# Column halves of the output summed in two TensorE column groups of one bank, two output stores, and w4 in five pieces

## The chip, the cores and the metric

One core of a Trainium2 chip runs the kernel. The metric is device time in microseconds (us) of one execution. Ratios are the mean time of one kernel's fast runs over the mean of the other's fast runs of the same rounds, so they are not quite the ratio of the medians quoted beside them. A profiled execution has a span (first to last instruction) about 1.8 us shorter than the time of the run.

## The reference

One decode step of a block: attention over the last 2,048 positions of a cache (4 batches, 32 query heads, 16 KV heads of 128), plus an MLP, both on the same normalised input, and a residual. What matters here is the last sum:

```python
def reference(...):
    xn = _layernorm(A_x)
    return A_x + attention(xn, K, V, wq) @ wo + mlp(xn, w1, w2, w3, w4)   # shortened
# mlp: x1 + gelu(layernorm(x1) @ w3) @ w4     w4: 4608 x 576, wo: 4096 x 576, output: 4 x 576
```

The weights and the cache window are 87 MB, read once, for 4 rows of output. (The sequence has one position, so the shifted part of the MLP is zero and the kernel leaves w1 and w2 out.)

## The kernel before

K, V, wo, w3 and w4 stream in on SyncE's DMA queue, and w4 comes last. The output is 4 x 576. TensorE's sums stand in PSUM, in banks; the widest matmul in this kernel's trace writes 512 columns, and the 576 columns here are summed as two halves of 288. A chunk is 128 rows of a weight (w4 has 36, wo 32). All wo terms (3 x 8 chunks during the loop and 8 at its end) and all 36 w4 chunks go into `acc`. The halves lie in different rows of the same 32-column group of TensorE: row `2 b + i` is half `i` of batch `b`, and the shifted view of a zero-padded `lhsT` with 8 columns puts half `i` into its rows.

```python
W4_PIECES = [0, NFH, NF - 12, NF - 6, NF - 2, NF - 1, NF]     # 0 18 24 30 34 35 36: six DMAs
...
second = []
def acc_matmuls(terms):
    for i in range(NI):                                       # NI = 2 halves
        for n, (lhsT, rhs) in enumerate(terms):
            to, q, start = (second[0], QD, second[1]) if second and n % 2 else (acc, 0, False)
            nc.tensor.matmul(out=to[q:q + OR, :], lhsT=lhsT[:, NI - 1 - i:NI - 1 - i + OR],
                             rhs=rhs[:, i * CW:(i + 1) * CW], start=start, stop=False, skip_group_check=True)
            ...
# the end of the kernel
acc_odd = ps_acc.tile([P, CW], F32, tag="g", name="acc_odd")  # a second bank, used by column group 1
second += [acc_odd, True]
...                                                            # last attention head
o_proj(hl)
mlp_out(*pieces[0]); ...; mlp_out(*pieces[3])                  # chunks 0 to 33: even -> acc, odd -> acc_odd
second.clear()
odd = const.tile([OR, CW], F32)
nc.scalar.activation(out=odd[:], in_=acc_odd[QD:QD + OR, :], func=ACT.Copy)
seen = const.tile([1, 1], F32)
nc.vector.tensor_copy(out=seen[:], in_=odd[0:1, 0:1])
for lo, hi in pieces[4:]:                                      # chunks 34 and 35, into acc alone
    mlp_out(lo, hi)
fin = const.tile([OR, CW], out.dtype)
nc.vector.tensor_tensor(out=fin[:], in0=acc[0:OR, :], in1=odd[:], op=ALU.add)
nc.sync.dma_start(out=o2.rearrange("b (i n) -> (b i) n", i=NI), in_=fin[:])
```

So in the closing stretch even and odd chunks already run side by side, in column groups 0 and 1, in two banks. Only the last two chunks run in one group, so that the odd sum can be copied out meanwhile.

## Time and profile before

| | before |
|---|---|
| time | 211.74 us (211.57 to 211.84, 3 runs) |
| span, mean granted clock | 209.9 us, 0.89 |
| DMA | 87.31 MB, mean 416 GB/s |
| last landing of w4 | 206.81 us |

From the page of the kernel before, the rows by 40 equal slices of the span. A digit is tenths of a slice; PEclk is the granted TensorE clock, DMA the mean busy share of the core's 16 DMA engines.

```profile
PE   0378198699670039649998999659995976898684
PEclk9999769999996557976999999999997968899969
DMA  8999999999999999999999999999999999999991
```

DMA is at 9 tenths or more from the second slice to the last but one; nothing else is. A change made under that stream cannot show unless it holds the stream up. What can show is the stream itself, and the stretch after its last byte.

The end of the chain of waits of the kernel before (start, length, what), with lines left out:

```profile
168.46 32.19 DMA w_sb<-in_B_w_dram
200.65 0.04 issue
200.70 0.40 PE acc L183
...
206.13 0.27 PE acc L183
...
206.81 0.41 ACT odd L612
207.22 0.02 issue
207.25 0.14 DVE seen L614
```

One w4 transfer, then TensorE to 206.8, then the odd sum. Taken alone it says that TensorE ended the stream. The landings say more. The trace records 16 increments of a semaphore for each of the six transfers; the last of the 16 is called its landing here. The six pieces landed at 200.65, 202.57, 204.69, 206.07, 206.43 and 206.81 us. The timeline of the kernel before (start, length, engine, line, operation, output, inputs, shape, count), in its last stretch:

```profile
206.12 0.29 PE L183 MATMUL acc_odd<-w_sb,gT 128*8 128x288 bf16 x1
206.24 0.28 PE L183 MATMUL acc<-w_sb,gT 128*8 128x288 bf16 x1
206.24 0.29 PE L183 MATMUL acc_odd<-w_sb,gT 128*8 128x288 bf16 x1
...
206.60 0.65 PE L183 MATMUL acc<-w_sb,gT 128*8 128x288 bf16 x4
206.81 0.40 ACT L612 ACTIVATE odd<-acc_odd 8x288 f32<-8x288 f32 x1 [10.46 <-PE acc_odd L183]
207.25 0.14 DVE L614 COPY seen<-odd 1x1 f32<-1x1 f32 x1 [8.54 <-ACT odd L612]
207.32 0.43 DVE L619 TENSOR_TENSOR fin<-acc,odd 8x288 bf16<-8x288 f32 x1
207.78 0.37 SPq L620 DMA_DIRECT2D out_dram<-fin  x1
```

Matmuls start at 200.70, 206.12 and (the third of the four in the line at 206.60) 206.85, each 0.04 us after a landing. So it is the landings that TensorE follows at the end. `acc` and `acc_odd` matmuls start together, 0.12 us from pair to pair (a "slot"). The windows of the kernel before (stretch, length, busy us of PE, PEld, DVE, ACT and POOL, then granted clock, DMA share, GB/s) show that half of this stretch ran at half clock:

```profile
197.00:200.50 3.50, 1.56 (x25) 0.97 (x24) 1.14 (x3) 0.00 (x0) 0.00 (x0) 1.00 0.93 388
200.50:204.00 3.50, 3.30 (x28) 1.90 (x29) 0.00 (x0) 0.00 (x0) 0.00 (x0) 0.51 1.01 422
204.00:206.00 2.00, 2.00 (x34) 1.47 (x31) 0.00 (x0) 0.00 (x0) 0.00 (x0) 1.00 0.71 272
206.00:207.50 1.50, 1.25 (x16) 0.63 (x11) 0.26 (x2) 0.40 (x1) 0.00 (x0) 1.00 0.11 39
```

The clock came back just in time for TensorE to catch up with the stream.

### The profile page before, as it was taken

To read this page: it belongs to the slowest core of one execution; us is meant where nothing else is said; L and a number is where in the kernel's file an instruction comes from. 1 tells how busy PE (TensorE), PEld (TensorE's weight loads), DVE (VectorE), ACT (ScalarE), POOL (GpSimd) and SP (SyncE) were. 2 spreads that over 40 slices of the span, in tenths; PEclk is the share of its full clock that TensorE was granted. 3 is DMA by queue.
4 is the path that set the end of the run, shared out by engine and by line. 5 is a ranking of instruction groups with operands and counts; after the bars stand their busy time and mean duration, and the time that the engine had idled before them with its cause. 6 is when DMAs were issued, how large, how long until landed. Compare 5 with 4: busy or idle time off the path is not lost.

```text
span 209.9 us, 2326 instructions
## 1 busy us (share of the span) xinstructions
PE 149.1 (71%) x941; PEld 60.2 (29%) x955; DVE 113.7 (54%) x165; ACT 34.4 (16%) x66; POOL 8.9 (4%) x33
## 2 busy tenths in 40 slices
PE   0378198699670039649998999659995976898684
PEld 0123032233220013223454333224331312343353
DVE  3611877985910084917507898465949391755200
ACT  7612201021120001111120312110111111113100
POOL 4620000000000000000000300000000000000000
PEclk9999769999996557976999999999997968899969
DMA  8999999999999999999999999999999999999991
GB/s 294 406 403 440 422 428 431 437 425 432 448 429 419 421 437 421 447 418 437 434 425 437 418 426 439 434 423 440 418 431 437 422 433 431 434 428 446 417 399 71
DMA packets 6658, 87.31 MB, mean 416 GB/s; under 512 B 748, under 2 KB 1016, under 8 KB 1656
## 3 DMA queue, kind: packets, MB, share of 16 engines
q1 hardware_dynamic: 6640, 87.17, 97.5%
q8 instruction: 7, 0.11, 0.2%
q10 hardware_dynamic: 8, 0.00, 0.0%
q14 instruction: 3, 0.02, 0.0%
HBM read 87.17 MB, written 0.00 MB: 415 GB/s over the span
## 4 chain that ended last, share of the span: by engine, by line
DMA 52%; PE 24%; DVE 19%; issue 2%; ACT 1%; SPq 0%; DVEq 0%; ACTq 0%
DMA vn<-in_A_v_cache_dram 19%; DMA w_sb<-in_B_w_dram 15%; DVE kt L226 14%; DMA kn<-in_A_k_cache_dram 12%; PE S L342 9%; DMA wq_sb<-in_A_wq_dram 6%; PE acc L183 4%; PE O L394 2%; PE g_ps L460 2%; PE q_ps L286 2%; DVE mx L348 2%; PE S L364 1%; PE oT L407 1%; DVE PT L376 1%; DVE dm L350 1%
## 5 line engine op out<-in xcount | busy, mean ns | idle before, releaser
L342 PE MATMUL S<-kt,qz 128*128 128x512 bf16 x242 | 74.0, 429 | 34.5 <-DVE kt L226 31.3
L226 DVE STREAM_TRANSPOSE kt<-kn 128x2048 int32<-128x2048 int32 x32 | 73.4, 2295 | 26.5 <-DMA kn<-in_A_k_cache_dram 25.0
L342 PEld LDWEIGHTS <-qz 128*128 128x128 bf16 x256 | 24.0, 108 | 63.5 <-issue 46.6
L394 PE MATMUL O<-vn,PT 128*32 128x512 bf16 x256 | 22.9, 400 | 8.4 <-DMA vn<-in_A_v_cache_dram 8.4
L370 ACT ACTIVATE E<-S 128x512 bf16<-128x512 f32 x16 | 9.5, 597 | 97.7 <-PE S L364 97.7
L376 DVE STREAM_TRANSPOSE PT<-E 128x512 bf16<-128x512 bf16 x16 | 11.4, 710 | 15.5 <-ACT E L370 15.5
L401 ACT ACTIVATE O_sb<-O,rd 128x512 f32<-128x512 f32 x16 | 11.0, 686 | 37.1 <-PE O L394 37.1
L394 PEld LDWEIGHTS <-PT 128*32 128x32 bf16 x256 | 5.9, 94 | 29.6 <-issue 28.6
L417 DVE TENSOR_REDUCE on<-oT 128x8 bf16<-128x128 f32 x16 | 4.6, 287 | 16.7 <-PE oT L407 16.6
L348 DVE TENSOR_REDUCE mx<-S 128x1 f32<-128x512 f32 x16 | 10.5, 658 | 1.2 <-PE S L342 1.1
L407 PE MATMUL oT<-ident_w,O_sb 128*128 128x128 f32 x64 | 11.0, 296 | 0.3 <-ACT O_sb L401 0.3
L407 PEld LDWEIGHTS oT<-ident_w,O_sb 128*128 128x128 f32 x64 | 7.0, 146 | 4.6 <-issue 3.9
L183 PE MATMUL acc<-wo_sb,op 128*8 128x288 bf16 x56 | 7.5, 286 | 1.0 <-DVE op L439 1.0
L364 PE MATMUL S<-nm,j_row 8*128 8x512 bf16 x16 | 6.3, 393 | 1.9 <-DVE nm L360 1.7
L183 PE MATMUL acc<-w_sb,gT 128*8 128x288 bf16 x38 | 6.6, 342 | 0.8 <-DMA w_sb<-in_B_w_dram 0.8
L380 PE MATMUL dn<-rs,same_j 128*128 128x1 f32 x32 | 6.4, 268 | 0.0
L380 PEld LDWEIGHTS dn<-rs,same_j 128*128 128x128 f32 x32 | 5.2, 204 | 4.1 <-issue 3.4
L330 PE MATMUL S<-negbig,ohT 4*128 4x512 bf16 x16 | 6.1, 384 | 0.0
L183 PE MATMUL acc_odd<-w_sb,gT 128*8 128x288 bf16 x34 | 6.1, 350 | 0.0
L183 PEld LDWEIGHTS <-op 128*8 128x8 bf16 x64 | 4.6, 87 | 3.2 <-DVE op L439 1.1
L286 PE MATMUL q_ps<-wq_sb,xnT 128*32 128x512 bf16 x40 | 4.5, 630 | 1.3 <-DMA wq_sb<-in_A_wq_dram 1.3
L478 DVE COPY g_x<-gT_ps 128x64 f32<-128x64 f32 (+1 forms) x3 | 0.6, 194 | 8.5 <-PE gT_ps L472 8.5
(93 smaller groups left out, 80.7 us busy)
## 6 DMA issues: line engine op xcount, KB each, us to landing
kn<-in_A_k_cache_dram SPq DMA_DIRECT2D x16, 2048.0 KB, 23.8
vn<-in_A_v_cache_dram SPq DMA_DIRECT2D x16, 2048.0 KB, 25.6
wo_sb<-in_A_wo_dram SPq DMA_DIRECT2D x4, 1152.0 KB, 26.4
w_sb<-in_B_w_dram SPq DMA_DIRECT2D x1, 4608.0 KB, 33.2
wq_sb<-in_A_wq_dram SPq DMA_DIRECT2D x1, 4096.0 KB, 12.8
w_sb<-in_B_w_dram SPq DMA_DIRECT2D x1, 2592.0 KB, 32.2
w_sb<-in_B_w_dram SPq DMA_DIRECT2D x2, 864.0 KB, 34.0
w_sb<-in_B_w_dram SPq DMA_DIRECT2D x2, 576.0 KB, 32.5
```

The costliest lines, as they stand in the source:

```text
L183: nc.tensor.matmul(out=to[q:q + OR, :], lhsT=lhsT[:, NI - 1 - i:NI - 1 - i + OR], rhs=rhs[:, i * CW:(i + 1) * CW], start=start, stop=False ...
L226: nc.vector.transpose(out=kt[:], in_=src)
L286: nc.tensor.matmul(out=q_ps[r][g * QD:(g + 1) * QD, :], lhsT=xnT[:, k, :], rhs=wq_sb[:, col:col + NW], start=(j == 0), stop=False, skip_gr ...
L342: nc.tensor.matmul(out=S_ps[h][:], lhsT=qz[:, z0:z0 + P], rhs=kt[:, ib, c0:c0 + SC, e:2 * QD:2].rearrange("p c k -> p (c k)"), start=False ...
L348: nc.vector.reduce_max(out=mx[:], in_=S_ps[h][:], axis=AX.X)
L364: nc.tensor.matmul(out=S_ps[h][:], lhsT=j_row[:], rhs=st.pop(("nm", h))[:, 0:1].to_broadcast([NJ, NW]), start=False, stop=False, skip_grou ...
L370: nc.scalar.activation(out=E[h][:].rearrange("p c k -> p (c k)"), in_=S_ps.pop(h)[:], func=ACT.Exp, scale=scale, accum_out=rs[:])
L376: nc.vector.transpose(out=PT[h][:], in_=E.pop(h)[:])
L380: nc.tensor.matmul(out=dn[:], lhsT=same_j[:], rhs=st.pop(("rs", h))[:], start=True, stop=True)
L394: nc.tensor.matmul(out=O_ps[h][g * QD:(g + 1) * QD], lhsT=PT[h][:, c, :], rhs=vn[:, :, c, :], start=(s == 0), stop=False, skip_group_check ...
L401: nc.scalar.activation(out=O_sb[h][:], in_=O_ps.pop(h)[:], func=ACT.Copy, scale=st.pop(("rd", h))[:, 0:1])
L407: nc.tensor.transpose(out=oT[:, s, :], in_=o[:, s, :], identity=ident_w[:, s * NJ:s * NJ + P])
```

## The change

The two halves of each chunk go to two column groups, at partitions 0 and 32 of the same bank. No zero-padded operands are needed, no odd sum, no second bank. The copy `fin` then has its rows in partitions 0 to 3 and 32 to 35. The check before the chip refuses one DMA for both (its access pattern may select partitions only in the first dimension), so there are two stores, on SyncE's and ScalarE's queues. With the odd sum gone, w4's second and third pieces are joined.

```diff
-    W4_PIECES = [0, NFH, NF - 12, NF - 6, NF - 2, NF - 1, NF]
+    W4_PIECES = [0, NFH, NF - 6, NF - 2, NF - 1, NF]
...
-    gT = cleared([P, NF, OW], "gT")
-    op = cleared([P, WOR, OW], "op")
+    gT = const.tile([P, NF, B], BF16, name="gT")
+    op = const.tile([P, WOR, B], BF16, name="op")
...
     def acc_matmuls(terms):
-        for i in range(NI):
-            for n, (lhsT, rhs) in enumerate(terms):
-                to, q, start = (second[0], QD, second[1]) if second and n % 2 else (acc, 0, False)
-                nc.tensor.matmul(out=to[q:q + OR, :], lhsT=lhsT[:, NI - 1 - i:NI - 1 - i + OR],
-                                 rhs=rhs[:, i * CW:(i + 1) * CW], start=start, stop=False, skip_group_check=True)
-                if start:
-                    second[1] = False
+        for lhsT, rhs in terms:
+            for i in range(NI):
+                nc.tensor.matmul(out=acc[i * QD:i * QD + B, :], lhsT=lhsT, rhs=rhs[:, i * CW:(i + 1) * CW],
+                                 start=False, stop=False, skip_group_check=True)
...
-    odd = const.tile([OR, CW], F32)
-    nc.scalar.activation(out=odd[:], in_=acc_odd[QD:QD + OR, :], func=ACT.Copy)
-    seen = const.tile([1, 1], F32)
-    nc.vector.tensor_copy(out=seen[:], in_=odd[0:1, 0:1])
-    for lo, hi in pieces[4:]:
+    for lo, hi in pieces:
         mlp_out(lo, hi)
 
-    fin = const.tile([OR, CW], out.dtype)
-    nc.vector.tensor_tensor(out=fin[:], in0=acc[0:OR, :], in1=odd[:], op=ALU.add)
-    nc.sync.dma_start(out=o2.rearrange("b (i n) -> (b i) n", i=NI), in_=fin[:])
+    fin = const.tile([P, CW], out.dtype)
+    nc.vector.tensor_copy(out=fin[:], in_=acc[:])
+    for i, eng in enumerate((nc.sync, nc.scalar)):
+        eng.dma_start(out=o2[:, i * CW:(i + 1) * CW], in_=fin[i * QD:i * QD + B, :])
```

Cut: the padded identity of the first term, and the same edits where `op`, `gT` and their callers use the padded rows.

More of the change, by code (lines that the diff above doesn't have):

```diff
@@ L166 @@
     qz = cleared([P, ZP + Hkv * 4 * P], "qz")
-    OR = NI * B
-    OW = OR + NI
-    ROWS = slice(NI - 1, NI - 1 + OR, NI)
-    gT = cleared([P, NF, OW], "gT")
-    op = cleared([P, WOR, OW], "op")
+    gT = const.tile([P, NF, B], BF16, name="gT")
+    op = const.tile([P, WOR, B], BF16, name="op")
     acc = ps_acc.tile([P, CW], F32)
     nc.vector.memset(acc[:], 0.0)
-    second = []
     def acc_matmuls(terms):
-        for i in range(NI):
-            for n, (lhsT, rhs) in enumerate(terms):
-                to, q, start = (second[0], QD, second[1]) if second and n % 2 else (acc, 0, False)
-                nc.tensor.matmul(out=to[q:q + OR, :], lhsT=lhsT[:, NI - 1 - i:NI - 1 - i + OR],
-                                 rhs=rhs[:, i * CW:(i + 1) * CW], start=start, stop=False, skip_group_check=True)
-                if start:
-                    second[1] = False
+        for lhsT, rhs in terms:
+            for i in range(NI):
+                nc.tensor.matmul(out=acc[i * QD:i * QD + B, :], lhsT=lhsT, rhs=rhs[:, i * CW:(i + 1) * CW],
+                                 start=False, stop=False, skip_group_check=True)
     def layernorm(dst_f, dst_bf, src):
@@ L268 @@
     nc.vector.reduce_sum(out=own[:], in_=ident_f[:].rearrange("p (h d) -> p h d", h=WOH), axis=AX.X)
-    idz = const.tile([B, OW], F32)
-    nc.gpsimd.memset(idz[:], 0.0)
-    nc.gpsimd.tensor_copy(out=idz[:, ROWS], in_=ident_f[0:B, 0:B])
     xsum = xn_f
     nc.gpsimd.tensor_tensor(out=xsum[:], in0=xn_f[:], in1=x_bf[:], op=ALU.add)
-    acc_matmuls([(idz[:], xsum)])
+    acc_matmuls([(ident_f[0:B, 0:B], xsum)])
     ln2_bf = part(D, B)
@@ L438, in o_pick @@
         with nc.allow_low_precision("one term is not zero"):
-            nc.vector.reduce_sum(out=op[:, :, ROWS], in_=mk[:].rearrange("p i h b -> p i b h"), axis=AX.X)
+            nc.vector.reduce_sum(out=op[:], in_=mk[:].rearrange("p i h b -> p i b h"), axis=AX.X)
     def o_proj(h):
@@ L443, in o_proj @@
             return
-        for i in range(0, WOR, 2):
-            acc_matmuls([(op[:, i + u, :], wo_tiles[h // WOQ][:, i + u, :]) for u in range(2)])
+        acc_matmuls([(op[:, i, :], wo_tiles[h // WOQ][:, i, :]) for i in range(WOR)])
     G_CHUNKS = [(e, 4 * g, 4) for e in range(2) for g in range(NQD)] + [(e, 16, 2) for e in range(2)]
@@ L486, in mlp_act @@
         nc.gpsimd.tensor_scalar(out=u[:], in0=u[:], scalar1=0.5, scalar2=0.5, op0=ALU.mult, op1=ALU.add)
-        nc.gpsimd.tensor_tensor(out=gT[:, :, ROWS], in0=u[:], in1=xs[:], op=ALU.mult)
+        nc.gpsimd.tensor_tensor(out=gT[:], in0=u[:], in1=xs[:], op=ALU.mult)
     def mlp_out(lo, hi):
         w4 = w_tiles["w4"]
-        for i in range(lo, hi, 2):
-            acc_matmuls([(gT[:, u, :], w4[:, u, :]) for u in range(i, min(i + 2, hi))])
+        acc_matmuls([(gT[:, u, :], w4[:, u, :]) for u in range(lo, hi)])
     order = [("K", 0), ("K", 1), ("K", 2)]
@@ L598 @@
     pieces = list(zip(W4_PIECES, W4_PIECES[1:]))
-    acc_odd = ps_acc.tile([P, CW], F32, tag="g", name="acc_odd")
-    second += [acc_odd, True]
     o_turn(hl)
@@ L605 @@
     o_proj(hl)
-    mlp_out(*pieces[0])
-    mlp_out(*pieces[1])
-    mlp_out(*pieces[2])
-    mlp_out(*pieces[3])
-    second.clear()
-    odd = const.tile([OR, CW], F32)
-    nc.scalar.activation(out=odd[:], in_=acc_odd[QD:QD + OR, :], func=ACT.Copy)
-    seen = const.tile([1, 1], F32)
-    nc.vector.tensor_copy(out=seen[:], in_=odd[0:1, 0:1])
-    for lo, hi in pieces[4:]:
+    for lo, hi in pieces:
         mlp_out(lo, hi)
-    fin = const.tile([OR, CW], out.dtype)
-    nc.vector.tensor_tensor(out=fin[:], in0=acc[0:OR, :], in1=odd[:], op=ALU.add)
-    nc.sync.dma_start(out=o2.rearrange("b (i n) -> (b i) n", i=NI), in_=fin[:])
+    fin = const.tile([P, CW], out.dtype)
+    nc.vector.tensor_copy(out=fin[:], in_=acc[:])
+    for i, eng in enumerate((nc.sync, nc.scalar)):
+        eng.dma_start(out=o2[:, i * CW:(i + 1) * CW], in_=fin[i * QD:i * QD + B, :])
 _INS = ['A_x', 'A_k_cache', 'A_v_cache', 'A_wq', 'A_wo', 'B_x', 'B_w1', 'B_w2', 'B_w3', 'B_w4']
```

## The prediction

> **What bounds the kernel now.** The page's slices show DMA at 9 tenths nearly everywhere, mean 416 GB/s; the chain of waits is 52% DMA, from 168.5 us one w4 transfer, then tail. The trace's semaphore landings put the six w4 pieces at 200.65, 202.57, 204.69, 206.07, 206.43 and 206.81 us, and the timeline shows matmuls starting 0.04 us after three of them (200.70, 206.12, 206.85). TensorE ran at half clock from 200.6 to 204.0 (windows view: 0.50), but had caught up: the last landing rules the end. After it (timeline):
> - the last chunk's two halves, one after the other in one column group: 206.85 to 207.26
> - fin, 8x288, 0.43 us, to 207.75
> - output DMA issued 207.78, landed 209.04; end protocol to 209.9.
>
> **What the change does.**
> 1. Column packing. Before, even and odd chunks already ran side by side (a pair per 0.12 us at full clock, 0.24 at half); only the last two chunks, after the odd sum was closed, and the three early output projections ran in one group. After, each chunk's halves run side by side, in one bank. The Trainium skill ("PSUM — Partial Sum Buffer", on bank collisions) says different column tiles may access one bank at once; this trace agrees: 16 PV matmuls of 512 columns, four groups of one bank, took 1.05 us. So w4 takes 36 slots, not 38; only the last chunk's is exposed: -0.12 us.
> 2. Odd's ScalarE copy (0.40 us, 206.81 to 207.21) and "seen" (0.14, to 207.39) go. The copy ran under the last matmuls and fin started 0.06 us after the last one: worth 0 to 0.05 us. The new fin copies 128x288; by DVE's 658 ns at 512 columns and 194 at 64 I estimate 0.43 us, unchanged.
> 3. Five w4 pieces: 256 packets of 6,912 bytes (262 ns) become 128 of 13,824 (estimate 517 ns, from packets of 16,384 and 20,736 bytes): 0.06 us less per engine, so the last landing comes that much earlier. Against it, chunks 18 to 29 wait until about 204.65; 12 slots end at 206.1, four more at 206.6, one at 206.75: just in time at full clock.
> 4. Two output DMAs of 4 rows. Issue took 0.37 us on SyncE, the early ScalarE one 0.55. The later of the two decides; I allow +0.1 us, partly returned by fewer descriptors each.
> 5. Prologue: two ScalarE clears (0.33, 0.22 us) and two POOL operations go; q waits for wq (landed 14.07) anyway: 0. The three early projections lose about 1 us of TensorE each, under DMA time: 0.
>
> Sum: -0.12 -0.06 -0.03 +0.07, about -0.15 us.
>
> **Prediction: 211.6 us, range 211.1 to 212.0.** Faster by over 2%: 0.005; within 2%: 0.99; slower by over 2%: 0.005.
>
> **What would show it.** Right: acc matmuls in pairs in the last two chunks; last w4 landing near 206.75 with the last matmul right behind; fin about 0.43 us; ScalarE's output issue the later. Wrong: halves one after the other (0.24 us per chunk at full clock), which would make TensorE the end, +4 us.
>
> **What would make it wrong.** The clock window: if half clock falls on 204.7 to 207, the bigger second piece leaves 18 chunks at 0.24 us after it, ending near 209: +1 to 2 us. The skill ("TensorE: Matmul & The Clock Gate", Part 1) calls that window free-running, so it may differ between executions; here lowered stretches last 3.41 us or multiples. A slow ScalarE issue would erase the gain.

## The result, and the profile after

| | before | after |
|---|---|---|
| time, same rounds | 211.79 us median (211.57 to 212.02, 4 runs) | 211.66 us median (211.53 to 211.96, 4 runs) |
| ratio | | 0.9996, interval 0.9978 to 1.0013 |
| span | 209.89 us | 209.83 us |

The medians differ by 0.13 us; the interval reaches well over both sides of 1. The page of the changed kernel, the same slices:

```profile
PEclk9999799999696557979999999669997895799699
```

The DMA row is the same, digit for digit. The end of the chain of waits of the changed kernel:

```profile
169.04 35.54 DMA w_sb<-in_B_w_dram
204.58 0.04 issue
204.62 2.40 PE acc L177 x36
207.02 0.02 issue
207.05 0.46 DVE fin L595
```

And its timeline:

```profile
199.87 1.15 PE L177 MATMUL acc<-wo_sb,op 128*4 128x288 bf16 x16 [0.97 <-DVE op L428]
200.85 2.37 PE L177 MATMUL acc<-w_sb,gT 128*4 128x288 bf16 x36
204.62 2.38 PE L177 MATMUL acc<-w_sb,gT 128*4 128x288 bf16 x36 [1.40 <-DMA w_sb<-in_B_w_dram]
207.05 0.46 DVE L595 CAST fin<-acc 128x288 bf16<-128x288 f32 x1 [7.23 <-PE acc L177]
207.53 0.34 SPq L597 DMA_DIRECT2D out_dram<-fin  x1
207.54 0.28 ACTq L597 DMA_DIRECT2D out_dram<-fin  x1
```

Eighteen chunks (36 matmuls) take 2.4 us, so a chunk's two halves take one slot of 0.12 us, in one bank. TensorE waits 1.40 us for the joined piece. The landings of the five pieces are 200.48, 204.58, 205.98, 206.36 and 206.68 us, and the last pair of matmuls starts at 206.72. That pair waited only 0.02 us: the pair before it started at 206.58, and one slot later is 206.70. So the 18 slots behind the joined piece, and the last landing, end almost together here too (the experiment `fourteen` pulls them apart). The windows of the changed kernel show full clock after 200.5:

```profile
197.00:200.50 3.50, 2.15 (x27) 1.51 (x27) 1.43 (x4) 0.17 (x1) 0.00 (x0) 0.88 0.98 412
200.50:204.00 3.50, 2.72 (x46) 1.84 (x41) 0.00 (x0) 0.00 (x0) 0.00 (x0) 1.00 0.92 391
204.00:206.00 2.00, 1.38 (x24) 1.01 (x24) 0.00 (x0) 0.00 (x0) 0.00 (x0) 1.00 0.70 269
206.00:207.50 1.50, 1.01 (x18) 0.62 (x12) 0.45 (x1) 0.00 (x0) 0.00 (x0) 1.00 0.06 21
```

Now the stretch after the stream, cut into stages. "Issue" is the start of the first store's issue, "landed" the last semaphore raised by a store.

| stage, us | before | after | difference |
|---|---|---|---|
| last w4 landing | 206.81 | 206.68 | -0.13 |
| from there to the store's issue | 0.97 | 0.86 | -0.11 |
| from issue to landed | 1.26 | 1.45 | +0.20 |
| from landed to the end of the span | 0.86 | 0.84 | -0.01 |
| span | 209.89 | 209.83 | -0.06 |

The stores give back most of what is won before them. The two parts of that win are not equally firm. The 0.11 us from the landing to the issue repeat (0.97 here and in before_two_stores, which has the same code up to the store; 0.86 in all three profiles of the changed kernel). The 0.13 us of the landing do not: the other three profiles of kernels with six pieces have it at 206.66, 206.70 and 206.81 us, the seven with five pieces at 206.61 to 206.71. The two landings are 0.18 us apart: ScalarE's store at 208.81, SyncE's, issued 0.004 us before it, at 208.98.

### The profile page after: what moved, and what is told of

Same layout as the page of the kernel before. It is cut to its first block, busy times and chain, and to the rows that moved or that the text cites. A ratio compares the mean times of both kernels' runs of the same rounds, so it can differ in the third digit from the quotient of the medians.

```text
span 209.8 us, 2321 instructions
## 1 busy us (share of the span) xinstructions
PE 146.2 (70%) x941; PEld 58.0 (28%) x955; DVE 114.0 (54%) x164; ACT 33.7 (16%) x63; POOL 8.7 (4%) x31
## 4 chain that ended last, share of the span: by engine, by line
DMA 77%; DVE 12%; PE 7%; ACT 1%; SPq 1%; issue 0%; DVEq 0%; ACTq 0%
DMA kn<-in_A_k_cache_dram 54%; DMA w_sb<-in_B_w_dram 17%; DVE kt L218 10%; DMA wq_sb<-in_A_wq_dram 6%; PE S L331 2%; PE q_ps L275 2%; PE acc L177 1%; DVE mx L337 1%; PE O L383 1%; DVE qz L307 1%; ACT q_sb L286 1%; DVE dm L339 0%; PE oT L396 0%; ACT qz L305 0%; SPq L141 0%
## 5 line engine op out<-in xcount | busy, mean ns | idle before, releaser
L383 PE MATMUL O<-vn,PT 128*32 128x512 bf16 x256 | 24.4, 425 | 11.6 <-DMA vn<-in_A_v_cache_dram 11.6
L396 PE MATMUL oT<-ident_w,O_sb 128*128 128x128 f32 x64 | 12.6, 333 | 0.0
L396 PEld LDWEIGHTS oT<-ident_w,O_sb 128*128 128x128 f32 x64 | 8.2, 165 | 5.2 <-issue 4.7
L177 PE MATMUL acc<-w_sb,gT 128*4 128x288 bf16 x72 | 4.8, 286 | 1.4 <-DMA w_sb<-in_B_w_dram 1.4
L275 PE MATMUL q_ps<-wq_sb,xnT 128*32 128x512 bf16 x40 | 3.8, 548 | 2.2 <-DMA wq_sb<-in_A_wq_dram 2.2
L177 PE MATMUL acc<-wo_sb,op 128*4 128x288 bf16 x64 | 4.6, 286 | 1.0 <-DVE op L428 1.0
L448 PE MATMUL g_ps<-w_sb,ln2T 128*32 128x512 bf16 (+1 forms) x50 | 4.9, 444 | 0.0
L595 DVE CAST fin<-acc 128x288 bf16<-128x288 f32 x1 | 0.5, 458 | 7.2 <-PE acc L177 7.2
```

The costliest lines, as they stand in the source:

```text
L177: nc.tensor.matmul(out=acc[i * QD:i * QD + B, :], lhsT=lhsT, rhs=rhs[:, i * CW:(i + 1) * CW], start=False, stop=False, skip_group_check=True)
L275: nc.tensor.matmul(out=q_ps[r][g * QD:(g + 1) * QD, :], lhsT=xnT[:, k, :], rhs=wq_sb[:, col:col + NW], start=(j == 0), stop=False, skip_gr ...
L383: nc.tensor.matmul(out=O_ps[h][g * QD:(g + 1) * QD], lhsT=PT[h][:, c, :], rhs=vn[:, :, c, :], start=(s == 0), stop=False, skip_group_check ...
L396: nc.tensor.transpose(out=oT[:, s, :], in_=o[:, s, :], identity=ident_w[:, s * NJ:s * NJ + P])
```

## The experiments

Theory A: the last landing of w4 and a fixed sequence after it set the time. The change gains 0.06 us of packets and one slot after the landing, and pays for its second store. Rival B: TensorE and the odd sum set the time, so the packing pays in full. Rival C: the difference is drift. Every ratio is to the kernel before on the same chip in the same rounds; one_group and one_group_again, and the two joined versions, ran on different chips.

### after_again: the changed kernel, five rounds

Edit: none.

> The changed kernel once more, unedited, for a closer interval and a second profile. Theory A (the last landing of w4 rules, the change shortens only what lies around it): 0.1 to 0.25 us below the kernel before on the same chip, ratio 0.9988 to 0.9995; last matmul pair starts within 0.1 us of the last w4 landing; store issue about 0.25 us earlier than before, counted from the last landing no more than 0.15 us earlier. Rival B (TensorE work and the odd sum rule, so packing should pay for all it saves, 0.24 us of slots plus 0.5 us of odd and seen): 0.5 us or more below. Rival C (what was seen is drift): no difference, 1.0000 within 0.0005.

Measured: 211.60 us (211.49 to 212.00, 5 runs) against 211.61 of before; ratio 1.0002 (0.9989 to 1.0014). The profile repeats the first one to 0.02 us: last landing 206.70, issue 0.86 later, landed 1.44 after that, span 209.84.

Rival B falls: 0.5 us would be a ratio of 0.9976, outside the interval. Theory A's 0.9988 to 0.9995 is inside the interval, but so is no difference at all. The stages before the store are reproducible; the gain in time is not shown.

### six_pieces: the changed kernel with w4 in six pieces

```diff
-    W4_PIECES = [0, NFH, NF - 6, NF - 2, NF - 1, NF]
+    W4_PIECES = [0, NFH, NF - 12, NF - 6, NF - 2, NF - 1, NF]
```

> The changed kernel with w4 in six pieces as before (12 chunks of the second piece again 6 and 6), all else changed. Theory A: packets of w4 per engine sum to 0.064 us more, so the last landing and the end come about 0.06 us later than in the changed kernel; the wait for chunk 18 ends about 2 us earlier (near 202.5) without any gain. Rival (the bigger piece makes TensorE wait and costs): the time falls by 0.5 us or more against the changed kernel.

Measured: 211.80 us (211.65 to 212.16), ratio to before 1.0012 (1.0000 to 1.0025); so about 0.2 us above the changed kernel beside it, and not 0.5 us below. The packets of w4 sum to 12.63 us per engine in place of 12.57, as expected. But the last landing came at 206.70, as in the changed kernel, and the end 0.5 us later. The windows of this profile say why:

```profile
197.00:200.50 3.50, 2.15 (x20) 1.46 (x20) 1.43 (x4) 0.04 (x1) 0.00 (x0) 0.50 0.90 378
200.50:204.00 3.50, 3.50 (x34) 1.90 (x32) 0.00 (x0) 0.00 (x0) 0.00 (x0) 0.52 1.00 419
...
206.00:207.50 1.50, 1.41 (x24) 0.77 (x18) 0.05 (x1) 0.00 (x0) 0.00 (x0) 1.00 0.08 28
```

Half clock from 193.6 to 203.9, three stretches of 3.41 us. TensorE was busy without a pause from 199.9 to 207.4, so in this execution it, not the landing, ended the stream, 0.4 us later than in the changed kernel (207.43 against 207.02). This is the edge that the profile before stood near. The number of pieces need not be its cause: the joined version below fell over it too, with five. So 0.2 us in the mean cannot be put down to the pieces.

### two_on_sync: both stores on SyncE's queue

```diff
-    for i, eng in enumerate((nc.sync, nc.scalar)):
+    for i, eng in enumerate((nc.sync, nc.sync)):
```

> The changed kernel with both output stores on SyncE's queue. Theory A: the second issue follows the first, about 0.34 us later, and its landing comes later by as much: 0.3 us slower than the changed kernel. Rival (issue is hidden in the latency of the write): less than 0.1 us.

Measured: 211.74 us (211.50 to 212.11), ratio 1.0007 (0.9993 to 1.0020). In the profile the second issue starts 0.40 us after the first (207.54 and 207.94), and the second store lands at 209.11, 0.36 us after the first (208.75). The store stage is 1.57 us, 0.12 to 0.13 above that with two queues, not 0.3. Span 209.97 in place of 209.83. The first of the two alone landed 1.21 us after its issue. So a single store of 4 rows needs 1.21 us, and the second costs 0.23 us on another queue and 0.36 on the same.

### before_five: the kernel before with five pieces

```diff
-    W4_PIECES = [0, NFH, NF - 12, NF - 6, NF - 2, NF - 1, NF]
+    W4_PIECES = [0, NFH, NF - 6, NF - 2, NF - 1, NF]
...
-    mlp_out(*pieces[3])          # the odd sum still ends at chunk 33
...
-    for lo, hi in pieces[4:]:
+    for lo, hi in pieces[3:]:
```

> The kernel before with w4 in five pieces, nothing else changed. Theory A: 0.06 us below the kernel before (0.9997), too small to be told from noise by the time, but the packets of w4 per engine sum to 12.57 us in place of 12.63; the last chunk's halves still one after the other, 0.12 us apart, after the last landing. Rival B: if packing did it all, exactly as before.

Measured: 211.76 us (211.70 to 211.82), ratio 1.0007 (0.9995 to 1.0020). Packets 12.57 us per engine as expected, last landing 206.65. Still it did not end earlier (span 209.89): the joined piece lands at 204.54, and from there 16 chunks in pairs and the last two in one group take 20 slots without a pause; the last four start at 206.53, 206.66, 206.78 and 206.90. The last two need the last landing but start 0.13 us after it, not 0.04: they stand in TensorE's queue. So the issue of the store comes 1.07 us after that landing in place of 0.97. The expectation missed this: joining the pieces is free only together with the packing, which takes two slots away.

### one_group and one_group_again: no second column group at all

```diff
-    acc_odd = ps_acc.tile([P, CW], F32, tag="g", name="acc_odd")
-    second += [acc_odd, True]
...
-    odd = const.tile([OR, CW], F32)
-    nc.scalar.activation(out=odd[:], in_=acc_odd[QD:QD + OR, :], func=ACT.Copy)
-    seen = const.tile([1, 1], F32)
-    nc.vector.tensor_copy(out=seen[:], in_=odd[0:1, 0:1])
...
-    nc.vector.tensor_tensor(out=fin[:], in0=acc[0:OR, :], in1=odd[:], op=ALU.add)
+    nc.vector.tensor_copy(out=fin[:], in_=acc[0:OR, :])
```

> The kernel before without its odd sum: no second column group, every half of every chunk goes one after the other into one group, six pieces, one store. Theory A (two groups are needed so that TensorE keeps up with the landings, and beyond that they gain nothing): the w4 stream needs 72 slots of 0.12 us from about 200.8, so at full clock the last matmul ends near 209.5, and each 3.41 us stretch of half clock adds 1.7: 2.2 to 5 us slower than the kernel before. Rival D (the last landing rules whatever TensorE does): within 0.5 us of the kernel before.

Measured: 215.59, 214.06 and 214.57 us; ratio 1.0150 (1.0122 to 1.0179), that is 3.2 us above the kernel before. One run took 264.45 us, and it was the profiled one, so the kernel was run once more:

> The one-group kernel once more, for a profile at the ordinary clock (the first profile fell in a run of 264 us). Theory A: TensorE, not the last landing near 206.8, ends the stream: matmuls 0.12 us apart at full clock without a wait for a landing, the last near 209.5 to 211.

Measured: 214.15 us, one run, state unknown. From the timeline of that profile:

```profile
200.74 8.98 PE L183 MATMUL acc<-w_sb,gT 128*8 128x288 bf16 x72
209.76 0.45 DVE L613 CAST fin<-acc 8x288 bf16<-8x288 f32 x1 [11.04 <-PE acc L183]
```

72 halves in 8.98 us, one per 0.12 us, at full clock and without a wait. The last landing was at 206.81; TensorE ended 2.9 us later. Rival D falls. Two column groups are what lets TensorE follow the stream. The kernel before had them already, and that is why the change had so little left to win.

### late_piece: more work behind a landing

```diff
-    W4_PIECES = [0, NFH, NF - 6, NF - 2, NF - 1, NF]
+    W4_PIECES = [0, NFH, NF - 2, NF - 1, NF]
```

> The changed kernel with w4 in four pieces, the second now chunks 18 to 33, so that 16 chunks may start only at about 205.95 with the landing of its end. Theory A: 18 slots of 0.12 us stand after that landing; last matmul ends near 208.3 in place of 207.0: 1.3 us slower than the changed kernel at full clock, up to 3.4 us if TensorE, idle from about 203 to 206, is put at half clock. Rival (a bigger piece is only fewer packets): 0.03 us faster.

Measured: 213.45 us (213.26 to 215.70), ratio 1.0121 (1.0073 to 1.0169). The profile is at full clock there. From the chain of waits:

```profile
169.28 36.73 DMA w_sb<-in_B_w_dram
206.01 0.04 issue
206.05 2.39 PE acc L177 x36
208.44 0.02 issue
208.46 0.46 DVE fin L595
```

The last matmul ends 1.4 us later than in the changed kernel (expected 1.3). The span grew by 1.92 us; the other 0.5 us stand after the store's landing, where this profile took 1.36 us to the end in place of 0.84. One of SyncE's closing semaphore steps starts 0.47 us after the one before it. In the kernel before a gap of 0.48 us stands among those steps too, but at 208.27 to 208.75, while the store is still under way, so it costs nothing there. What causes the gap is open. The run of 215.70 would fit half clock after 206 (an estimate: 18 slots of 0.24 in place of 0.12 us are 2.2 us more), but its trace was not kept.

### fourteen: more packets

```diff
-    W4_PIECES = [0, NFH, NF - 6, NF - 2, NF - 1, NF]
+    W4_PIECES = list(range(0, NF - 3, 3)) + [NF - 3, NF - 2, NF - 1, NF]
```

> The changed kernel with w4 in 14 pieces (eleven of three chunks, three of one). Packets of 3,456 bytes are estimated at 136 ns from those of 1,152 (51 ns) and 4,608 (178 ns): w4 takes 13.17 us per engine in place of 12.57. Theory A: the last landing, and the end with it, come 0.6 us later than in the changed kernel (ratio to the kernel before near 1.0028). Rival (packet count does not matter, the byte rate does): no change, or a gain from smaller waits.

Measured: 212.23 us (212.04 to 212.52), ratio 1.0033 (1.0019 to 1.0046). Packets of w4: 13.16 us per engine (expected 13.17). The last landing came at 207.15, 0.47 us later than in the changed kernel, with the last pair of matmuls 0.04 us behind it; the span grew by 0.55 us. From the chain of waits:

```profile
200.84 6.31 DMA w_sb<-in_B_w_dram
207.15 0.04 issue
207.19 0.30 PE acc L177 x2
```

Here TensorE was not at its limit: the pair before started at 206.83, so TensorE waited 0.24 us beyond a slot before the last one. This is the run that shows the last landing to rule by itself. The rival falls: with the same bytes, more packets push the last landing, and the end goes with it.

### before_two_stores: the kernel before with its store cut in two

```diff
-    nc.sync.dma_start(out=o2.rearrange("b (i n) -> (b i) n", i=NI), in_=fin[:])
+    for e, eng in enumerate((nc.sync, nc.scalar)):
+        eng.dma_start(out=o2.rearrange("b (i n) -> (b i) n", i=NI)[e * B:(e + 1) * B, :], in_=fin[e * B:(e + 1) * B, :])
```

> The kernel before with its one output store of 8 rows cut into two of 4 rows on SyncE's and ScalarE's queues, all else as before. Theory A (two stores on two queues cost time): the later landing comes 1.44 us after the issue in place of 1.26, with the two landings 0.18 us apart, so about 0.19 us slower than the kernel before (1.0009). Rival (the longer store of the changed kernel comes from reading partitions 0 and 32 or writing half rows): 1.26 us as before, time the same.

Measured: 211.73 us (211.63 to 211.96) against 211.52; ratio 1.0010 (0.9997 to 1.0022), so +0.2 us with an interval that just reaches 1. In the profile the two stores are issued together:

```profile
207.62 0.35 SPq L621 DMA_DIRECT2D out_dram<-fin  x1
207.63 0.28 ACTq L621 DMA_DIRECT2D out_dram<-fin  x1
```

They land at 208.82 and 209.00, 0.18 us apart as in the changed kernel; the stage takes 1.38 us in place of 1.26. After the landing the end took 0.98 us in place of 0.86: SyncE checks its semaphores one after another, and one more check stood behind the last landing. So the second store costs 0.12 us by itself and up to 0.12 more by where its check falls. The rival (partition 32, half rows) falls for the larger part: the gap of 0.18 us is there with whole rows from partitions 0 to 7. The changed kernel's stage is 0.07 us longer still, and that rest is not explained.

The order of landing fits what the Trainium skill says ("DMA: Bandwidth & Descriptors", Queues, rings and completion order): both queues run on the same DMA engines, and a semaphore increment is a strongly ordered write, across queues. The later store's four increments come 0.17 to 0.18 us after the other store's, engine by engine (changed kernel: 208.66, 208.69, 208.74, 208.81 and 208.84, 208.86, 208.91, 208.98), although its data had been written only 0.03 to 0.06 us later. That this ordering is the cause is argued, not shown.

### joined and joined_busy: keep the gain, drop the second store

The second half sums in a bank of its own, so VectorE and ScalarE can copy the two halves out at the same time, into one tile of 4 rows, which one DMA stores. (With both halves in one bank the built program makes ScalarE's copy wait for VectorE's; no run was made of that.) The bank is found by moving the gate's sums elsewhere.

```diff
     acc = ps_acc.tile([P, CW], F32)
+    acc1 = ps_acc.tile([P, CW], F32, tag="acc1", name="acc1")         # and cleared
...
-                nc.tensor.matmul(out=acc[i * QD:i * QD + B, :], ...
+                nc.tensor.matmul(out=(acc, acc1)[i][i * QD:i * QD + B, :], ...
...
-        g_ps = ps_acc.tile([P, P, n], F32, tag="g", name="g_ps")
+        g_ps = (ps_o if r < 2 else ps_m).tile([P, P, n], F32, tag="O" if r < 2 else "m", name="g_ps")
...
-    fin = const.tile([P, CW], out.dtype)
-    nc.vector.tensor_copy(out=fin[:], in_=acc[:])
-    for i, eng in enumerate((nc.sync, nc.scalar)):
-        eng.dma_start(out=o2[:, i * CW:(i + 1) * CW], in_=fin[i * QD:i * QD + B, :])
+    fin = const.tile([B, D], out.dtype)
+    nc.vector.tensor_copy(out=fin[:, 0:CW], in_=acc[0:B, :])
+    nc.scalar.activation(out=fin[:, CW:D], in_=acc1[QD:QD + B, :], func=ACT.Copy)
+    nc.sync.dma_start(out=o2, in_=fin[:])
```

> A version that should keep what the change gains and drop what it pays: column halves side by side and five pieces as in the changed kernel, but the second half sums in a bank of its own (the gate's sums of the MLP move to other banks), so that VectorE and ScalarE may copy the two halves out at once into one tile of 4 rows of 576, stored by one DMA. Theory A (the change wins about 0.12 us after the last landing and 0.06 us of packets, and pays 0.19 us for the second store): store issued 0.85 us after the last landing as in the changed kernel, landed 1.21 to 1.26 us after its issue in place of 1.45: 0.2 us below both kernels in the profile (span near 209.6), ratio near 0.9990. Rival C (nothing but drift): the same as both; or the moved gate sums cost something near 105 us, which should be hidden under the DMA.

Measured: 211.68 us (211.47 to 211.93) against 211.55; ratio 1.0000 (0.9986 to 1.0014). The profiled run was the slowest (211.93), and again half clock lasted to 203.8: the last matmul ended 0.74 us after the last landing, in place of 0.33. The store stage did shrink, to 1.30 us. A miss in the time.

Beside it ran the changed kernel a third time:

> The changed kernel unedited a third time, on the chip of the joined version. Theory A with the stores counted (gains 0.18, pays 0.19): no difference to the kernel before, ratio 0.9996 to 1.0004 in the mean over all its rounds; two landings 0.18 us apart, the later 1.45 us after the issue, again.

Measured: 211.64 us (211.44 to 212.25), ratio 1.0008 (0.9995 to 1.0021); the mean lies a little above the expected band. The stages are those of the other two profiles: last landing 206.68, issue 0.86 later, landed 1.44 after that, the two landings 0.18 apart.

Last, the joined version with TensorE kept busy in the idle gaps before the end:

```diff
+    def busy(n):                       # sums into rows that nobody reads
+        for _ in range(n):
+            nc.tensor.matmul(out=acc[2 * QD:2 * QD + B, :], lhsT=gT[:, 0, :], rhs=wo_tiles[hl // WOQ][:, 0, 0:CW],
+                             start=False, stop=False, skip_group_check=True)
+    busy(8)                            # before the last PV; busy(5) before, busy(4) after the last projection
```

> The joined version with 17 matmuls more, whose sum goes to rows that nobody reads, put into TensorE's idle gaps before the last PV (8), before the last projection (5) and after it (4), to keep the clock up near the end. Theory E (part of the spread, and of what the joined version and the six-piece version lost, is half clock lasting until about 203.8, after which TensorE ends the w4 stream later than its landing): full clock in the windows from 197 to 207, last matmul ends within 0.5 us of the last landing, no run above 211.75, ratio to the kernel before near 0.9990 (211.4). Rival (the spread comes from elsewhere; clock near the end is without effect, or the added matmuls delay the last projection): spread and mean as in the joined version, ratio 1.0000 or above.

Measured: 211.57 us (211.40 to 211.77) against 211.54; ratio 1.0001 (0.9988 to 1.0015). The windows of this profile:

```profile
197.00:200.50 3.50, 2.25 (x36) 1.32 (x36) 1.14 (x3) 0.00 (x0) 0.00 (x0) 1.00 0.96 404
200.50:204.00 3.50, 2.35 (x36) 1.58 (x36) 0.00 (x0) 0.00 (x0) 0.00 (x0) 1.00 0.96 406
```

Full clock in these and in the two windows up to 207.5, and the last matmul ends 0.33 us after the last landing. But the time did not fall to 211.4, and one run was at 211.77. Stages: last landing 206.71, issue 0.89 later, landed 1.30 after that, end 0.94 later (again with one more check of SyncE behind the landing), span 209.84. What the stages before gain, 0.18 us, comes back as 0.04 in the store and 0.09 in the end. Whether the added matmuls kept the clock up, or this execution had it up anyway, one profile cannot tell. None of these versions beats the kernel before beyond the intervals.

## Why the prediction was right, and where it was off

The time, 211.66 us against 211.6 predicted, lies inside the range and near its middle, and "within 2%" was right. Over all its rounds, though, the changed kernel's 14 runs average 211.70 us and the kernel before's 22 runs beside them 211.63. In the three sets of rounds the difference of the means was -0.09, +0.04 and +0.17 us. So the predicted gain of 0.15 us is not confirmed as a gain; it is smaller than the runs can tell, and that the first medians differ by 0.13 us is luck.

1. **The last landing rules the end: right, but by a hair.** Five profiles of five-piece kernels have the last matmul pair within 0.05 us of the last landing (three of the changed kernel, two_on_sync and joined_busy), but TensorE's own queue ended within 0.02 us of it in the two main profiles, so these alone don't tell the two apart. Fourteen pieces do: landing and end moved together there, with TensorE waiting; late_piece moved the end by the slots behind a landing. It holds only while TensorE keeps up: six_pieces and joined show executions in which half clock until 203.8 made TensorE the end, 0.4 us late. The prediction named the clock window as its risk, for the stretch from 204.7 to 207; what was seen is an earlier stretch with a smaller cost.
2. **Packing: right.** Halves in two groups of one bank run together, one slot of 0.12 us per chunk. Predicted -0.12 us from the last landing to the store, measured -0.11. That the three early projections gain nothing is argued from the full DMA rows, not shown apart.
3. **The odd sum was almost free: right.** Rival B, under which it would pay, is outside the interval.
4. **Five pieces: right in size.** Packets of 6,912 bytes (264 ns on average) became packets of 13,824 (520 ns); the sum per engine fell from 12.63 to 12.57 us, 0.06 as predicted. From the first piece's landing to the last one's, as means over the 16 increments, it is 6.29 to 6.30 us in four profiles with six pieces and 6.24 to 6.25 in seven with five: 0.05 us, clear of the scatter. The last landing itself came 0.13 us earlier; about 0.07 of that was there before (the first piece, the same in both kernels, landed 0.07 us earlier in that mean), and it did not repeat. The expectation of before_five, that joining is free without the packing too, was wrong.
5. **The stores: mis-sized.** The term was +0.07 net. It measured +0.20 from issue to landing. The reason given was wrong too: ScalarE's issue is the shorter one (0.28 us, not 0.55 as early in the kernel), and its store landed first; SyncE's lands 0.18 us after it. Cutting the store of the kernel before in two reproduces the 0.18 us.

Put together: -0.13 (0.06 of it from the change) -0.11 +0.20 -0.01 gives, before rounding, the -0.06 us of the span. That the sum fell on the predicted side is luck: drift in the stream covered part of what the stores cost more. With only the 0.06 us of the packets in place of the 0.13, the same stages add up to about nothing.

## What to carry to other kernels

When a kernel is bound by one stream of loads, cost a change to its end by the stages after the last landing, each read from the trace; a saving in an engine that already keeps up with the landings is worth only what stands behind the last of them. Count the output stores: two stores issued together do not land together, and a layout that needs a second one can give back what it gained. When the expected effect is a tenth of a per cent, judge by stages, check on further profiles that each one repeats, and say that the time cannot decide.

## What the Trainium skill lacked or had wrong

- "DMA: Bandwidth & Descriptors" says that the two hardware queues share the DMA engines and that semaphore increments are ordered across queues, but gives no cost of a second queue's store. Here two small stores issued 0.004 us apart on SyncE's and ScalarE's queues landed 0.18 us apart in all seven profiles that had two such stores, the one issued first landing last.
- The same page ("Why small descriptors are slow") names a fixed overhead per packet and works it out for 256 bytes, not for packets of kilobytes. Here it shows there too: 51 ns at 1,152 bytes and 178 ns at 4,608, a straight line with about 9 ns at zero bytes, and w4 in 14 pieces in place of 5 took 13.16 us per engine in place of 12.57.
- "TensorE: Matmul & The Clock Gate" (Part 1) ties half clock to an idle window; its section on a second failure mode speaks of frequent short idle times, but gives no busy share. In the kernel before, half clock followed a window (197.0 to 200.5) in which TensorE was busy 1.56 of 3.5 us, so a partly busy window was enough; joined_busy, with 2.25 us busy there, kept full clock. What share is needed, no run here settles.
- No fault here: "PSUM — Partial Sum Buffer" (PSUM bank collisions) says that column tiles may access one bank at the same time; the changed kernel's pairs, 0.12 us apart in one bank, agree.
- No page has the time from the last store's landing to the end of the program's own instructions: 0.84 to 0.98 us in thirteen of the fourteen profiles here, and 1.36 in one.
- Open, and no fault of a page: the execution of 264.45 us (one_group). Its profile has no clock records, so its granted clock reads 1.00, while 72 matmuls took 19.15 us in place of 8.98. It is unexplained.
